# Wide key projections, shorter S words and a moved constant in a polysketch attention and expert kernel

## The chip, the cores and the metric

The kernel runs on one core of a Trainium2 chip. The metric is the device time of one execution in microseconds (us). A ratio is the mean time of one kernel's runs over the mean of the other kernel's runs of the same rounds, so it is not quite the ratio of the medians that are quoted.

## The reference, cut to what matters

```python
def phi(x):                                   # per head, R = 8
    a = np.einsum('rd,bhsd->bhsr', S1, x)
    b = np.einsum('rd,bhsd->bhsr', S2, x)
    return outer_product(a, b)                # 64 features
kv  = phi(k).T @ v ;  z = phi(k).sum(over s)
num = phi(q) @ kv  ;  den = phi(q) @ z + 1e-06
x   = (num / den), heads side by side         # 4352 x 128
# then four experts, gated: out += p[:, e] * (relu(x @ w1[e]) @ w2[e])
```

Batch 4, heads 4, sequence 1088, head dimension 32; the experts have 1024 hidden columns. S1 and S2 arrive as float64, so the kernel builds for each a leading float32 (hi) and a rest (lo) out of the bits, and projects with both.

## The kernel before

TensorE (PE) holds the 128x128 array as two halves of 64 columns and gives each half its own matmul in turn (`on_side`). The experts fill nearly all of PE's time. The attention of the next batch is cut into small "pieces" that are put between the experts' matmuls. Batch 0's keys and the first 128 rows run alone at the start, since nothing else can run yet.

The key projection, four tiles of 128 keys at a time, adds hi and lo in PSUM:

```python
for t in range(n):
    for i in range(2):              # hi, lo
        for _ in range(2):          # the two halves
            on_side(
                lambda s: _ap(kf, HP * s, HP, 32 * t, [[P, 2], [1, 32]]),
                lambda s: kT[:, P * (t0 + t) + HP * s : ... + HP],   # weights: 64 columns
                lambda s: sk[:, HP * i : HP * i + HP],               # moving: 64 columns
                start=(i == 0), stop=(i == 1))
nc.scalar.copy(<fss[b], both parts>, <kf>)
```

The first unit (`attend_first`) turns the denominators, adds 1e-6, takes the reciprocal, turns it back and multiplies:

```python
nc.vector.transpose(dT[:, 0:n], nd[0][:, 0:n])
nc.vector.tensor_scalar(out=rc, in0=<dT column>, scalar1=1e-6, scalar2=1.0, op0=ADD, op1=MULT)
nc.vector.reciprocal(rc, rc)
nc.vector.transpose(rb, <rc, repeated>)
nc.vector.tensor_tensor(out=xT, in0=nd[1], in1=rb, op=MULT)
```

Later units of queries write x to device memory and load it back turned (`xd<-y`, then `xT<-xd`); the experts of a chunk need that load.

## Time and profile before

| | before |
|---|---|
| median time | 491.54 us (491.28 to 491.69, 3 runs) |
| span of the profiled run | 489.5 us |
| first expert matmul starts | 14.16 us |
| last matmul ends | 486.15 us |
| between the two ("main part") | 471.99 us |

PE is busy in the main part but for one wait of 0.6 us. VectorE (DVE), ScalarE (ACT) and GpSimd (POOL) work beside it, so what matters is the start, the number of PE cycles in the main part, and the rare places where PE waits. The views are shown in the prediction.

### The profile page before, as it was taken

Reading aid. Unit: us, or ns where it says so; the run is one execution under the profiler, and the core shown is the slowest. Engines: PE = TensorE matmul, PEld = TensorE weight load, DVE = VectorE, ACT = ScalarE, POOL = GpSimd, SP = SyncE. Lnnn points to the kernel's source line nnn. Section 1 sums busy time; section 2 is a strip of 40 time slices with the busy share of each in tenths; the row PEclk is TensorE's granted clock in tenths of the full one; section 3 lists DMA queues with packets and bytes.
Section 4 is the critical chain, followed back from the end, with each engine's and each line's share of the span. In section 5 each row is a group of like instructions: output and inputs, shape, how many; then the busy total and the mean of one; then the engine's idle time right before and its main releaser. Section 6 shows DMA issues by size and latency. Waiting matters only on the chain.

```text
span 489.5 us, 11439 instructions
## 1 busy us (share of the span) xinstructions
PE 482.6 (99%) x4602; PEld 361.1 (74%) x4602; DVE 318.5 (65%) x746; ACT 244.4 (50%) x487; POOL 226.8 (46%) x260
## 2 busy tenths in 40 slices
PE   8999999999999999999999999999999999999997
PEld 5877777777767777555777777777777777878997
DVE  6759585868676757768675564575575666665642
ACT  3344463455445634535455464445455455566651
POOL 6052473516355444334555353444555355555570
PEclk9999999999999999999999999999999999999999
DMA  7990230040102520041102200031101200120000
GB/s 207 290 284 22 88 95 1 2 137 1 34 2 80 139 55 1 1 118 23 33 2 87 50 0 1 2 87 23 33 1 55 49 1 1 50 50 2 15 3 18
DMA packets 37588, 26.25 MB, mean 54 GB/s; under 512 B 26016, under 2 KB 34592, under 8 KB 37024
## 3 DMA queue, kind: packets, MB, share of 16 engines
q1 hardware_dynamic: 37520, 25.53, 19.0%
q8 instruction: 36, 0.59, 0.5%
q14 instruction: 16, 0.13, 0.1%
q10 hardware_dynamic: 16, 0.00, 0.0%
HBM read 21.28 MB, written 4.24 MB: 52 GB/s over the span
## 4 chain that ended last, share of the span: by engine, by line
PE 96%; DVE 2%; DMA 1%; issue 0%; ACT 0%; SPq 0%; DVEq 0%
PE h L188 49%; PE o L188 40%; PE f L188 4%; PE den L188 3%; DMA kn<-in_k_dram 1%; DVE qp L450 1%; DVE hid L698 1%; PE num L188 1%; PE h L176 0%; DVE kT L314 0%; ACT hid L723 0%; DVE qa L584 0%; ACT sh L842 0%; SPq L119 0%; DVE xT L486 0%
## 5 line engine op out<-in xcount | busy, mean ns | idle before, releaser
L188 PE MATMUL h<-xT,w_sb 128*64 128x512 f32 (+4 forms) x1408 | 300.2, 495 | 0.5 <-DVE xT L486 0.5
L698 DVE SCALAR_TENSOR_TENSOR hid<-h,hid 128x256 f32<-128x256 f32 (+6 forms) x432 | 203.6, 472 | 148.2 <-ACT hid L723 139.2
L723 ACT ACTIVATE hid<-h 128x512 f32<-128x512 f32 (+3 forms) x288 | 158.4, 550 | 195.0 <-PE h L188 157.0
L188 PE MATMUL o<-hid,w2s 128*64 128x256 f32 (+3 forms) x1152 | 221.6, 355 | 0.0
L188 PE MATMUL o<-hid,w_sb 128*64 128x256 f32 (+3 forms) x864 | 183.9, 355 | 0.0
L188 PEld LDWEIGHTS h<-xT,w_sb 128*64 128x64 f32 x1408 | 144.2, 137 | 51.8 <-issue 9.2
L188 PEld LDWEIGHTS o<-hid,w2s 128*64 128x64 f32 x1152 | 131.7, 137 | 30.9 <-issue 0.2
L838 POOL TENSOR_TENSOR ev<-yz,sh 64x256 f32<-64x256 f32 (+3 forms) x72 | 48.4, 672 | 163.5 <-ACT sh L841 160.8
L188 PEld LDWEIGHTS o<-hid,w_sb 128*64 128x64 f32 x864 | 101.0, 137 | 24.5 <-issue 6.3
L826 POOL TENSOR_TENSOR yz<-ev 128x512 f32<-128x512 f32 (+3 forms) x36 | 42.1, 1170 | 61.8 <-ACT ev L829 61.8
L838 POOL TENSOR_TENSOR ct<-ev 128x512 f32<-128x512 f32 (+3 forms) x36 | 42.0, 1167 | 2.8
L838 POOL TENSOR_TENSOR ct<-ct,gate 128x512 f32<-128x512 f32 (+3 forms) x27 | 32.1, 1189 | 2.1
L838 POOL TENSOR_TENSOR total<-total,ct 128x512 f32<-128x512 f32 (+3 forms) x27 | 31.8, 1179 | 2.1
L450 DVE TENSOR_TENSOR qp<-qa,qb 64x384 f32<-64x384 f32 (+3 forms) x44 | 32.1, 729 | 1.0
L828 ACT COPY ev<-o 128x512 f32<-128x512 f32 (+3 forms) x36 | 19.4, 539 | 11.3 <-PE o L188 10.8
L188 PE MATMUL o<-w_sb,hid 128*64 128x128 f32 x256 | 21.7, 273 | 0.0
L829 ACT COPY ev<-o 128x512 f32<-128x512 f32 (+3 forms) x36 | 19.4, 539 | 2.6
L715 ACT ACTIVATE hid<-h 128x256 f32<-128x256 f32 x24 | 9.2, 384 | 21.2 <-PE h L188 20.7
L188 PEld LDWEIGHTS o<-w_sb,hid 128*64 128x64 f32 x256 | 17.8, 137 | 2.1 <-issue 1.9
L353 DVE TENSOR_TENSOR kp<-fs 128x256 f32<-128x256 f32 (+1 forms) x24 | 14.7, 617 | 0.0
L841 ACT COPY sh<-yz 64x256 f32<-64x256 f32 (+3 forms) x36 | 13.7, 379 | 1.7 <-POOL yz L826 0.8
L842 ACT COPY sh<-yz 64x256 f32<-64x256 f32 (+3 forms) x36 | 13.7, 380 | 0.9
(113 smaller groups left out, 230.2 us busy)
## 6 DMA issues: line engine op xcount, KB each, us to landing
w_sb<-in_moe_w_dram SPq DMA_DIRECT2D x8, 512.0 KB, 7.5
gate<-gates SPq DMA_DIRECT2D x4, 1024.0 KB, 5.5
kn<-in_k_dram SPq DMA_DIRECT2D x4, 544.0 KB, 4.6
vn<-in_v_dram SPq DMA_DIRECT2D x16, 128.0 KB, 4.2
gate<-gates SPq DMA_DIRECT2D x2, 896.0 KB, 5.7
qn<-in_q_dram SPq DMA_DIRECT2D x3, 544.0 KB, 5.5
xd<-y SPq DMA_DIRECT2D x26, 48.0 KB, 1.7
out_dram<-ob SPq DMA_DIRECT2D x16, 64.0 KB, 2.0
```

Source lines behind the costliest of these rows:

```text
L188: nc.tensor.matmul(out(s), weights(s), moving(s), **flags)
L353: eng.tensor_tensor(out=_ap(kps[b], 0, P, 256 * t0 + P * p + 64 * x, [[256, n], [32, 2], [R, 4], [1, R]]), in0=_ap(src, 0, P, off + 4 * x, ...
L450: nc.vector.tensor_tensor(out=qp[p][64 * x : 64 * x + 64, 0:n], in0=qa[64 * p : 64 * p + 64, 0:n], in1=qb[64 * p : 64 * p + 64, 0:n], op=A ...
L698: nc.vector.scalar_tensor_tensor(out=out, in0=src, scalar=0.0, in1=in1, op0=ALU.max, op1=ALU.subtract)
L715: nc.scalar.activation(hd[:, 0 : 2 * n], hp[:, 0 : 2 * n], ACTF.Relu)
L723: nc.scalar.activation(hd[:, n * j : n * j + n], hp[:, 0:n], ACTF.Relu)
L826: add = lambda out, in0, in1, op=ALU.add: nc.gpsimd.tensor_tensor(out=out, in0=in0, in1=in1, op=op)
L828: nc.scalar.copy(_ap(ev, 0, P, 0, [[2 * w, 2], [1, w]]), _ap(a0, 0, P, 0, two))
L829: nc.scalar.copy(_ap(ev, 0, P, w, [[2 * w, 2], [1, w]]), _ap(a1, 0, P, 0, two))
L838: add = lambda out, in0, in1, op=ALU.add: nc.gpsimd.tensor_tensor(out=out, in0=in0, in1=in1, op=op)
L841: nc.scalar.copy(sh[HP:P, 0:w], yz[0:HP, 0, 0:w])
L842: nc.scalar.copy(sh[0:HP, 0:w], yz[HP:P, 1, 0:w])
```

## The change

Its intent is to take work off PE and off the serial start. Batches 1 to 3 project with hi and lo side by side as one 128-column moving operand, half as many matmuls, and VectorE adds the two results. The bits of S take twelve VectorE operations instead of fifteen, the copies of S are shared between ScalarE and GpSimd, and in the first unit 1e-6 enters the denominators through a matmul. One copy at the start changes place. The core of the diff:

```diff
+    def key_project_wide(b, gi, kf):
+        for t in range(n):
+            for _ in range(2):
+                on_side(
+                    lambda s: kf[half[s], P * t : P * t + P],
+                    lambda s: kT[:, P * (t0 + t) + HP * s : P * (t0 + t) + HP * s + HP],
+                    lambda s: sk[:, :],
+                    start=True, stop=True)
+        nc.scalar.copy(<fss[b]>, <hi columns of kf>)
+    def key_add(b, gi, kf):
+        nc.vector.tensor_tensor(out=fs, in0=<lo columns of kf>, in1=fs, op=ALU.add)
 ...   # keys(b): key_project -> key_project_wide, key_add one piece later
 ...   # attend_first:
+        if c == 0:
+            for _ in range(2):
+                on_side(lambda s: nd[0][half[s], 0:n],
+                        lambda s: _ap(vx, 0, P, D, [[0, HP]]),      # ones
+                        lambda s: _ap(eps, 0, P, 0, [[0, n]]),      # 1e-6 in one row
+                        start=True, stop=False)
-                    start=True,
+                    start=(i > 0 or c > 0),
+        if c:   # the tensor_scalar remains for later units only
 ...   # words: s_x, s_m, s_f by scalar_tensor_tensor (shift, then or)
 ...   # sk, sp, sr: copies split between ScalarE and GpSimd
 ...   # start():
         key_project(b, 0, kf[0])
+        key_project(b, 1, kf[1])
         next(value)
-        key_project(b, 1, kf[1])
```

More of the change, by code (lines that the diff above doesn't have):

```diff
@@ L170 @@
         nc.gpsimd.memset(own2[32 * h : 32 * h + 32, h % 2 : h % 2 + 1], 1.0)
+    eps = cpool.tile([P, 1], F32, name="eps")
+    nc.gpsimd.memset(eps[:, :], 0.0)
+    nc.gpsimd.memset(eps[0:1, :], 1e-6)
     def keep_warm(n):
@@ L200, in bits, with either @@
         nc.vector.tensor_scalar(out=out, in0=in0, scalar1=s1, scalar2=s2, op0=op0, op1=op1)
-    def either(out, a, b):
-        nc.vector.tensor_tensor(out=out, in0=a, in1=b, op=ALU.bitwise_or)
+    def either(out, in0, s1, op0, in1):
+        nc.vector.scalar_tensor_tensor(out=out, in0=in0, scalar=s1, in1=in1, op0=op0, op1=ALU.bitwise_or)
     low = _ap(s_raw, 0, R2, 0, [[2, D]])
@@ L214, with copy_on @@
     bits(s_m[:, lo], high, 31, shr, 31, shl)
+    bits(s_x[:, hi], high, 12, shl, 9, shr)
     bits(s_e[:, hi], s_f[:, hi], float(127 - 1023), ALU.add, 0.0, ALU.max)
     bits(s_e[:, lo], s_f[:, hi], float(127 - 1023 - 52), ALU.add, 0.0, ALU.max)
-    bits(s_x[:, hi], high, 12, shl, 9, shr)
-    bits(s_x[:, lo], low, 29, shr)
-    bits(s_n[:, hi], s_e[:, hi], 1.0, ALU.min)
+    either(s_x[:, hi], low, 29, shr, s_x[:, hi])
     bits(s_n[:, lo], low, 3, shl, 3, shr)
     bits(s_f[:, :], s_e[:, :], 255.0, ALU.min)
-    either(s_x[:, hi], s_x[:, hi], s_x[:, lo])
-    bits(s_e[:, :], s_f[:, :], 23, shl)
-    either(s_m[:, hi], s_x[:, hi], s_m[:, lo])
-    either(s_f[:, :], s_e[:, :], s_m[:, :])
+    either(s_m[:, hi], s_m[:, lo], 0, shl, s_x[:, hi])
+    bits(s_n[:, hi], s_e[:, hi], 1.0, ALU.min)
+    either(s_f[:, :], s_f[:, :], 23, shl, s_m[:, :])
     nc.vector.tensor_tensor(out=s_hl[0:R2, :], in0=s_n[:, :], in1=s_f[:, :].bitcast(F32), op=ALU.mult)
     nc.vector.transpose(s_T[:, :], s_hl[:, :])
+    def copy_on(scalar):
+        return nc.scalar.copy if scalar else nc.gpsimd.tensor_copy
     for h in range(H):
-        nc.scalar.copy(_ap(sk, 32 * h, 32, R2 * h, [[HP, 2], [1, R2]]), _ap(s_T, 0, 32, 0, [[D, 2], [1, R2]]))
+        copy_on(h < 2)(_ap(sk, 32 * h, 32, R2 * h, [[HP, 2], [1, R2]]), _ap(s_T, 0, 32, 0, [[D, 2], [1, R2]]))
     for i in range(3):
-        nc.gpsimd.tensor_copy(
+        copy_on(i == 2)(
             _ap(sp, 0, 32, HP * i, [[32, 2], [R, 4], [1, R]]),
@@ L240 @@
     for h in range(H):
-        nc.gpsimd.tensor_copy(
-            _ap(sr, 32 * h, 32, 32 * h, [[P, 6], [1, 32]]), _ap(sp, 0, 32, 0, [[32, 6], [1, 32]])
-        )
+        copy_on(h > 1)(_ap(sr, 32 * h, 32, 32 * h, [[P, 6], [1, 32]]), _ap(sp, 0, 32, 0, [[32, 6], [1, 32]]))
     mask_lo = [R2 + l % R2 for l in range(32)]
@@ L348, in key_project @@
         )
+    def key_project_wide(b, gi, kf):
+        t0, n = FG[gi]
+        if gi == 0:
+            fss[b] = apool.tile([P, 2, NT, 32], F32, tag="fs", name="fs")
+            kps[b] = apool.tile([P, NT, 2, P], F32, tag="kp", name="kp")
+        for t in range(n):
[4 more added lines that the diff above has]
+                    lambda s: sk[:, :],
+                    start=True,
+                    stop=True,
+                )
+        nc.scalar.copy(
+            _ap(fss[b], 0, P, 32 * t0, [[32 * NT, 2], [32, n], [1, 32]]), _ap(kf, 0, P, 0, [[32, 2], [P, n], [1, 32]])
+        )
+    def key_add(b, gi, kf):
+        t0, n = FG[gi]
+        fs = _ap(fss[b], 0, P, 32 * t0, [[32 * NT, 2], [32, n], [1, 32]])
+        nc.vector.tensor_tensor(out=fs, in0=_ap(kf, 0, P, HP, [[32, 2], [P, n], [1, 32]]), in1=fs, op=ALU.add)
     def key_product(b, t0, n, p, x, eng, kf=None):
@@ L397, in keys @@
             yield
+        kf = []
         for gi, (pool, tag) in enumerate(((ps_f, "f"), (ps_n, "den"), (ps_n, "num"))):
-            key_project(b, gi, psum(pool, tag))
+            kf.append(psum(pool, tag))
+            key_project_wide(b, gi, kf[gi])
+            if gi:
+                key_add(b, gi - 1, kf[gi - 1])
             yield
@@ L403, in keys @@
         for t0, n in ((0, 4), (4, 5)):
+            if t0:
+                key_add(b, 2, kf[2])
             for p in range(2):
@@ L460, in attend_first @@
         nd = [psum(ps_n, "den"), psum(ps_n, "num")]
+        if c == 0:
+            for _ in range(2):
+                on_side(
+                    lambda s: nd[0][half[s], 0:n],
+                    lambda s: _ap(vx, 0, P, D, [[0, HP]]),
+                    lambda s: _ap(eps, 0, P, 0, [[0, n]]),
+                    start=True,
+                    stop=False,
+                )
         for i in range(2):
@@ L474, in attend_first @@
         rc = apool.tile([P, QW // 32], F32, tag="rc", name="rc")
-        nc.vector.tensor_scalar(
-            out=rc[:, 0 : n // 32], in0=_ap(dT, 0, P, 0, [[32, n // 32]]), scalar1=1e-6, scalar2=1.0, op0=ALU.add, op1=ALU.mult
-        )
-        nc.vector.reciprocal(rc[:, 0 : n // 32], rc[:, 0 : n // 32])
+        column = _ap(dT, 0, P, 0, [[32, n // 32]])
+        if c:
+            nc.vector.tensor_scalar(
+                out=rc[:, 0 : n // 32], in0=column, scalar1=1e-6, scalar2=1.0, op0=ALU.add, op1=ALU.mult
+            )
+            column = rc[:, 0 : n // 32]
+        nc.vector.reciprocal(rc[:, 0 : n // 32], column)
         rb = apool.tile([P, UNITS[0][1]], F32, tag="rb", name="rb")
```

## The prediction

> **What bounds the kernel now.** I began with the page: busy times, then the chain that ended last.
>
> ```profile
> PE 482.6 (99%) x4602; PEld 361.1 (74%) x4602; DVE 318.5 (65%) x746; ACT 244.4 (50%) x487; POOL 226.8 (46%) x260
> ...
> PE 96%; DVE 2%; DMA 1%; issue 0%; ACT 0%; SPq 0%; DVEq 0%
> ```
>
> PE is busy for 99% and is 96% of the chain. Busy is not yet "at its rate", so I asked second for the waits of PE, and third for the instructions by form.
>
> ```profile
> PE h L176 <- DVE s_hl L212: 1.2, 1, 1.2
> PE h L188 <- DVE kT L314: 0.8, 1, 0.8
> PE den L188 <- DVE qp L450: 0.6, 1, 0.6
> PE h L188 <- DVE xT L486: 0.5, 1, 0.5
> PE den L188 <- DVE kvz L376: 0.5, 1, 0.5
> ```
>
> That is the whole list: 3.6 us, of which only the 0.6 us (a query sum at 200.35 us that waits for a product of VectorE) lies after 14.16 us. I also took each f32 form's usual start-to-start distance on one half of the array, summed these from 14.16 us on over the two halves, and got 470.2 us; from 14.16 us to the last matmul's end at 486.15 us is 472.0. So some 1.5 us at most of the main part is waiting, nearly all in the query sums. After 14.16 us only fewer PE cycles can help; before it, only what delays the first expert matmul. I read that part from the chain in order of time:
>
> ```profile
> 1.21 3.73 DMA kn<-in_k_dram
> ...
> 4.96 0.72 DVE kT L314
> ...
> 5.82 2.32 PE h L188 x72
> 8.14 0.88 PE o L188 x16
> 9.01 0.44 PE num L188 x8
> 9.45 2.12 PE f L188 x72
> ...
> 11.66 0.30 DVE kvz L376
> ...
> 12.01 0.44 PE den L188 x4
> ```
>
> Keys' load, their transposes, then solid PE from 5.82 to 11.57 us. What follows the denominators is best seen in VectorE's timeline (start, duration):
>
> ```profile
> 12.49 0.32 DVE L472 STREAM_TRANSPOSE dT<-den 128x128 f32<-128x128 f32 x1 [0.35 <-PE den L188]
> 12.85 0.17 DVE L475 TENSOR_SCALAR rc<-dT 128x4 f32<-128x4 f32 x1
> 13.05 0.18 DVE L478 RECIPROCAL rc<-rc 128x4 f32<-128x4 f32 x1
> 13.26 0.31 DVE L480 STREAM_TRANSPOSE rb<-rc 128x128 f32<-128x128 f32 x1
> 13.68 0.38 DVE L486 TENSOR_TENSOR xT<-num,rb 128x128 f32<-128x128 f32 x1
> ```
>
> This is one serial run of five operations; xT ends at 14.06 us and PE starts the first experts at 14.16. The chain view puts the 1 us before xT on the four keep-warm matmuls ("PE h L176"). I do not believe that: xT reads the numerators, done at 12.66 us, and the reciprocals, which came at 13.57 us.
>
> **What the Trainium skill says.** "Perfetto Trace Analysis", section "Identifying the Most-Contended Engine", warns that matmul busy time is a poor measure of distance to the limit. Hence my start-to-start sum; it agrees here that PE is full. "TensorE: Matmul & The Clock Gate", section "LDWEIGHTS (loading the stationary operand)", gives weight columns / 1.2 as ns: 53 ns for 64 columns. The trace fits a floor of about that size: a 64-column matmul record should take half of a 128-column one, but on one half of the array the starts are 58 ns apart against 109. That page's "Back-to-back issue gap" says the spacing is set by load and matmul together. "SBUF — State Buffer", section "Who interferes with whom", has a VectorE operation with at most one SBUF input, outside the two-port modes, not contend with GpSimd. The new sums read one PSUM and one SBUF operand. That no contention follows is not shown by the trace of before.
>
> **The change part by part.**
>
> *Wide key projections (batches 1 to 3 only; batch 0's start keeps the narrow ones).* Before, a batch has 9 tiles x 2 (hi, lo) x 2 halves = 36 matmuls of 64 columns, in the trace 72 records, f32 being recorded twice. After it has 18 matmuls of 128 columns, 36 records. The moving columns are the same; half the weight loads go. The spacing comes from these rows:
>
> ```profile
> 5.82 2.32 PE L188 MATMUL h<-sk,kT 128*64 128x64 f32 x72 [0.76 <-DVE kT L314]
> 7.94 0.31 PE L188 MATMUL o<-qT,sr 128*64 128x128 f32 x2
> ...
> 17.12 0.64 PE L188 MATMUL o<-w_sb,hid 128*64 128x128 f32 x8
> 17.56 0.64 PE L188 MATMUL h<-xT,w_sb 128*64 128x128 f32 x8
> ```
>
> 72 narrow records go from 5.82 to 7.94: 29.4 ns each with both halves working. Eight 128-column records go from 17.12 to 17.56: 0.437 us by the finer record, 54.7 ns each. Per batch 72 x 29.4 = 2.12 us becomes 36 x 54.7 = 1.97 us: 0.15 us saved, 0.44 us over three batches. It lies wholly on the PE path, so the end moves by it. This is small because hi and lo still cost their columns; the halved loads remove only the floor.
>
> *VectorE's additions.* New per batch: two of 128x256 and one of 128x64 from PSUM plus SBUF. The nearest rows are the start's products of the same operand kinds: 418 ns (128x256) and 211 ns (128x64). So 2 x 0.418 + 0.211 = 1.05 us, 3.1 us over three batches, taking VectorE from 318.5 to 321.6 us. ScalarE's copies keep their sizes (372, 372, 208 ns). All of it lies beside PE. VectorE's operations on hid idle 148 us before them, mostly for ScalarE, and the experts' second matmuls run two steps (some 6 us) behind the first, so half a microsecond in a step is absorbed. Path cost: 0.
>
> *1e-6 by a product, first unit only.* The tensor_scalar goes: from its start at 12.85 to the reciprocal's at 13.05 is 0.20 us on the serial run. Added are two 128-column matmuls into den, 4 x 54.7 = 0.22 us of PE. They need only constants and are issued after the key sums, so they run at 11.57 to 11.79 us, inside the 0.46 us in which PE waits for kvz. Net 0.20 us off the start.
>
> *Words in twelve operations.* Fifteen VectorE operations run from 2.47 to 4.44 us. Three fewer, at about 0.12 us a step (1.97 / 16 with the transpose), are 0.3 to 0.4 us. But VectorE then idles 0.52 us until the keys land at 4.94, so this only lengthens that wait: 0.
>
> *Copies of S shared between ScalarE and GpSimd.* sk is ready at 5.44 us before, sooner after. The first projection waits until 5.82 for kT. The sr copies end at 6.62 and are needed at 7.94. So 0.
>
> *Second projection's copy ahead of the first value copy.* VectorE idles 0.53 us for it before 8.70, so the products start sooner. But PE is solid through 11.57 us and the products are already in time: 0. The price is later value and qb copies on ScalarE: by its durations I get 8.95 instead of 8.41 us for the first value copy (needed at 9.25) and 10.4 instead of 9.65 for qb. The four query products, 0.29 us each, then end near 11.55 instead of 11.27, just ahead of kvz at 11.66. Up to 0.1 us of loss is possible here.
>
> Sum: 0.44 + 0.20 - 0.05 (expected part of that loss) = about 0.6 us of 491.54: 490.9.
>
> **The rivals.** First: the additions on VectorE delay hid work, PSUM banks come free later, and PE waits. For it: the three banks f, den, num are held longer, and an addition waits in the strict queue for ScalarE's copy, so hid behind it waits too. Against it: after 14 us the trace has one PE wait of consequence with VectorE at 65%, and the banks' next users come several pieces later. If each of nine additions cost PE 0.3 us, 2.7 us would go and the time would be about 493.6. Second: the start reorder backfires. If value or query copies come so late that PE's key sums stall or kvz is pushed, 0.2 to 0.5 us is lost and the gain is cancelled: 491.0 to 491.5. Third: the start gains more, because sk or the words were hidden limits on PE's first projection. The wait on kT speaks against it; at best 0.3 us more, 490.6. Fourth: the 1.5 us of query-sum waits shift, because all timing against the product pieces shifts; plus or minus 0.5 us either way.
>
> **Range and chances.** Small known terms of 0.6 us, jitter of 0.4 us between runs of before (491.28 to 491.69), and the fourth rival give 490.2 to 491.7. Two per cent would be 9.8 us: all that waits in PE is under 8 us, so faster by that is all but excluded. Slower by that would take a stall in every batch that no view hints at.
>
> **What would show it.** In the changed profile: PE projection records into f and den with 128 columns, 109 ns apart on a half, 36 per batch; PE busy lower by about 0.4 us; VectorE busy higher by 2 to 4 us; the first xT product starting near 13.48 and the first expert matmul near 13.95 us; PE's waits after that still near 0.6 us. I am wrong if the first expert matmul does not move (the keep-warm matmuls, or the query copies, set it after all), if new waits of PE for kf's banks or hid appear around 55, 155 and 275 us, or if 128-column records are spaced clearly over 109 ns.

## The result, and the profile after

| | before | after |
|---|---|---|
| median, 6 runs each | 491.51 us (491.28 to 491.89) | 490.64 us (490.54 to 491.0) |
| ratio | | 0.9983 (95%: 0.997 to 0.9996) |
| span of the profile | 489.5 us | 488.9 us |
| keys' first transpose starts | 4.96 | 5.20 |
| from it to the first expert matmul | 9.20 | 9.00 |
| main part | 471.99 | 471.24 |

The change is 0.87 us faster by the medians: inside the range, a little more than the 0.6 us that were forecast. It is far below 2%; the ratio's interval leaves out 1, but barely. The page of the changed kernel, busy time by engine and the chain by engine:

```profile
PE 482.5 (99%) x4498; PEld 358.8 (73%) x4498; DVE 322.1 (66%) x752; ACT 244.7 (50%) x488; POOL 226.6 (46%) x261
...
PE 96%; DVE 2%; DMA 1%; issue 0%; ACT 0%; SPq 0%; DVEq 0%
```

PE has 104 records fewer: 3 x 36 saved, 4 added for 1e-6. Its busy time falls by 0.1 us only, where the prediction looked for 0.4. Split by stage it does show the gain: 471.38 us become 470.63 in the main part, but the warm-up matmuls took 4.26 instead of 3.86 us in this profile, and the rest of the start 7.58 instead of 7.36, which is the product for 1e-6. VectorE's busy time rises by 3.6 us, of which the additions are 3.1. Groups of VectorE by form (count, busy us and mean ns, idle before):

```profile
L377 DVE TENSOR_TENSOR fs<-f,fs 128x256 f32<-128x256 f32 x3 | 1.2, 414 | 0.0
L377 DVE TENSOR_TENSOR fs<-den,fs 128x256 f32<-128x256 f32 x3 | 1.2, 414 | 0.0
...
L377 DVE TENSOR_TENSOR fs<-num,fs 128x64 f32<-128x64 f32 x3 | 0.6, 215 | 0.0
```

The serial run at the end of the start, in VectorE's timeline of the changed kernel:

```profile
12.73 0.32 DVE L516 STREAM_TRANSPOSE dT<-den 128x128 f32<-128x128 f32 x1 [0.34 <-PE den L193]
13.08 0.18 DVE L525 RECIPROCAL rc<-dT 128x4 f32<-128x4 f32 x1
13.29 0.31 DVE L527 STREAM_TRANSPOSE rb<-rc 128x128 f32<-128x128 f32 x1
13.71 0.38 DVE L533 TENSOR_TENSOR xT<-num,rb 128x128 f32<-128x128 f32 x1
```

From dT to xT's product it is 0.98 us now and was 1.19. The product starts at 13.71 although the last keep-warm matmul ends only at 13.87: the keep-warm matmuls, which the chain view of before had in this place, do not set it. The whole start is later in this profile all the same, since the keys landed 0.24 us later; the experiments show how far this moves by itself.

The projections themselves, PE's timeline of before around the first group of batch 3 (four tiles), and then of the changed kernel:

```profile
274.65 1.10 PE L188 MATMUL f<-sk,kT 128*64 128x64 f32 x29
275.59 0.38 PE L188 MATMUL o<-hid,w_sb 128*64 128x256 f32 x1
```

```profile
274.15 1.10 PE L193 MATMUL f<-sk,kT 128*64 128x128 f32 x15
275.03 0.38 PE L193 MATMUL o<-hid,w_sb 128*64 128x256 f32 x1
```

On the half that starts first, 16 narrow records take 0.94 us (58 ns each) and eight wide ones 0.88 (109 ns each). That is 0.06 us for four tiles, and by the finer starts 0.129 us for the nine tiles of a batch. Three times that is 0.39 us, but the main part is 0.75 us shorter. Where the other 0.36 us come from was the open question.

### The profile page after: what moved, and what is told of

Read it like the earlier page. It is cut to its first block, busy times and chain, and to the rows that moved or that the text cites. A ratio compares the mean times of both kernels' runs of the same rounds, so it can differ in the third digit from the quotient of the medians.

```text
span 488.9 us, 11239 instructions
## 1 busy us (share of the span) xinstructions
PE 482.5 (99%) x4498; PEld 358.8 (73%) x4498; DVE 322.1 (66%) x752; ACT 244.7 (50%) x488; POOL 226.6 (46%) x261
## 4 chain that ended last, share of the span: by engine, by line
PE 96%; DVE 2%; DMA 1%; issue 0%; ACT 0%; SPq 0%; DVEq 0%
PE h L193 49%; PE o L193 40%; PE f L193 4%; PE den L193 2%; DMA kn<-in_k_dram 1%; DVE qp L485 1%; DVE hid L745 1%; PE num L193 0%; PE h L181 0%; DVE kT L319 0%; ACT hid L770 0%; DVE qa L631 0%; ACT sh L889 0%; SPq L119 0%; DVE xT L533 0%
## 5 line engine op out<-in xcount | busy, mean ns | idle before, releaser
L485 DVE TENSOR_TENSOR qp<-qa,qb 64x384 f32<-64x384 f32 (+3 forms) x44 | 33.4, 758 | 1.0
```

The source lines that it names most:

```text
L485: nc.vector.tensor_tensor(out=qp[p][64 * x : 64 * x + 64, 0:n], in0=qa[64 * p : 64 * p + 64, 0:n], in1=qb[64 * p : 64 * p + 64, 0:n], op=A ...
```

## The experiments

Eleven kernels ran; all gave correct results. In the table, "start" is from the keys' first transpose to the first expert matmul, "main" from there to the last matmul's end, both in the one profile of that kernel.

| run | median (runs) | ratio to before (95%) | start | main |
|---|---|---|---|---|
| e1 wide only | 490.82 (5) | 0.9982 (0.9969 to 0.9994) | 9.20 | 471.24 |
| e2 1e-6 only | 491.30 (5) | 0.9993 (0.998 to 1.0005) | 9.00 | 471.86 |
| e3 words and copies only | 491.70 (5) | 0.9998 (0.9986 to 1.0011) | 9.20 | 472.07 |
| e4 order only | 491.56 (5) | 0.9997 (0.9983 to 1.0011) | 9.24 | 472.31 |
| e5 all but wide | 491.43 (5) | 0.9994 (0.998 to 1.0008) | 9.00 | 472.18 |
| e6 narrower still | 497.87 (4) | 1.0126 (1.0112 to 1.014) | 9.21 | 478.15 |
| e7 additions x 4 | 490.58 (4) | 0.9977 (0.9964 to 0.9991) | 9.44 | 470.91 |
| e8 before again | 491.77 (5) | 1.0003 (0.999 to 1.0015) | 9.71 | 472.38 |
| e9 before, shifted | 492.77 (4) | 1.0033 (1.0015 to 1.0052) | 9.51 | 471.83 |
| e10 after, shifted | 491.56 (4) | 0.9999 (0.9984 to 1.0014) | 9.70 | 471.24 |
| e11 sums later | 490.90 (6) | 0.9982 (0.997 to 0.9995) | 9.00 | 471.35 |

The medians of before in the same rounds were 491.56 (e1 to e4), 491.63 (e5 to e8), 491.69 (e9, e10) and 491.71 us (e11).

### Each part alone

e1 takes only the wide projections with their additions:

```diff
 ...   # key_project_wide and key_add as in the change
-            key_project(b, gi, psum(pool, tag))
+            kf.append(psum(pool, tag))
+            key_project_wide(b, gi, kf[gi])
+            if gi:
+                key_add(b, gi - 1, kf[gi - 1])
```

> Only the wide key projections with their additions, the start as before. My theory: the whole gain of this part is on PE's path. 36 records of 128 columns at 109 ns on a half replace 72 of 64 columns at 58 ns: 0.13 to 0.15 us a batch, 0.4 us in all. The two traces so far suggest up to 0.75 us from the first expert matmul to the last matmul (471.99 us before, 471.24 after), so 0.4 to 0.75 us faster than before, and the start not earlier. Rival A (the start made most of the gain): 0 to 0.2 us faster. Rival B (the additions on VectorE hold PE up): slower, with new waits of PE in the three key stretches.

It was 0.74 us faster by the medians, the start stayed at 9.20 us and the main part was 471.24 us, exactly that of the changed kernel. Rivals A and B fall: the main part's whole gain is in this edit, and no new wait appeared.

e2 takes only the product for 1e-6:

```diff
+        if c == 0: <two matmuls of ones by eps into nd[0], start=True, stop=False>
-        nc.vector.tensor_scalar(out=rc, in0=<dT>, scalar1=1e-6, ...)
-        nc.vector.reciprocal(rc, rc)
+        nc.vector.reciprocal(rc, <dT>)          # c == 0 only
```

> Only the 1e-6 by a product in the first unit. My theory: 0.20 us faster, because one operation of 0.20 us from start to start leaves the serial run from the denominators to xT; from the end of the keys' load to the first expert matmul 9.0 us instead of 9.22. Rival (the keep-warm matmuls set the start of xT's product, as the chain view has it): 0, with xT's product still starting just after the fourth keep-warm matmul ends.

The start fell from 9.20 to 9.00 us and xT's product began at 13.77 us, before the last keep-warm matmul ended at 13.94. The time is 0.26 us lower, within its noise; the 0.20 us is what the trace shows.

e3 and e4 take the words with the copies, and the order of the copies:

```diff
-        nc.scalar.copy(<sk, h>)                 # e3: sk, sp and sr shared, words in twelve
+        copy_on(h < 2)(<sk, h>)
-        next(value)                             # e4
         key_project(b, 1, kf[1])
+        next(value)
```

> Only the words in twelve operations and the shared copies of S. My theory: 0 (within 0.1 us): the transposed S is ready some 0.4 us earlier, VectorE waits that much longer for the keys, and PE's first projection still follows the keys' transpose by 0.14 us. Rival A: the copies of sk were a hidden limit, then 0.2 to 0.4 us faster, with PE's first projection closer to the keys' transposes.

> Only the order at the start: second projection's copy ahead of the first value copy. My theory: 0 within 0.1 us: PE runs without a gap from the first projection to the last key sum, and the query products still end before kvz. Rival: it loses up to 0.1 us where the query products end later than PE's key sums, or gains where the key products held PE's key sums (then fewer us from the first projection to the last key sum than 5.75).

Both left the time where it was. In e3 the turned S was ready at 4.05 us instead of 4.44, and VectorE then waited 1.17 us for the keys instead of 0.52 (0.26 of it because they landed later in this profile). In e4 the query products ended at 11.45 us and kvz started at 11.89: the loss of up to 0.1 us that the prediction allowed for did not come.

e5 is the changed kernel with the narrow projections back:

```diff
-        kf = []
 ...
-            kf.append(psum(pool, tag))
-            key_project_wide(b, gi, kf[gi])
-            if gi:
-                key_add(b, gi - 1, kf[gi - 1])
+            key_project(b, gi, psum(pool, tag))
 ...   # and the last key_add goes too
```

> The changed kernel with only the wide projections undone (and the additions with them). My theory: 0.2 us faster than the kernel before (the product's part alone), so 0.4 to 0.75 us slower than the changed kernel. Rival A (the start made most of the gain): 0.6 to 0.9 us faster than before.

It kept the 0.20 us of the start (9.00) and lost the main part's gain: 0.20 us faster than before by the medians. So the parts add up. What e3, e4 and e5 also show is a main part between 472.07 and 472.31 us, longer than before's 471.99, while the two kernels with wide projections had 471.24 both times.

### The floor under a narrow matmul

e6 makes the narrow projections narrower, with the same columns in all:

```diff
+            for p in range(2):                            # batches 1 to 3
                 for i in range(2):
                     for _ in range(2):
-                        moving sk[:, HP * i : HP * i + HP]                # 64 columns
+                        moving sk[:, HP * i + 32 * p : HP * i + 32 * p + 32]   # 32 columns
```

> The kernel before with each 64-column key projection of batches 1 to 3 split into two of 32 columns: 72 matmuls, 144 records a batch, moving columns unchanged, results right. My theory (the load of the 64 weight columns sets a floor of some 58 ns on a half): the 32-column records are also about 58 ns apart, a batch costs 144 x 58 / 2 = 4.2 us instead of 2.1, and the kernel is 6.3 us slower. Rival (no floor, each record has a fixed cost of about 5 ns besides its columns, 53 ns for 64): 32 columns take 27 + 5 = 32 ns, a batch 2.3 us, and the kernel is 0.5 us slower.

The two theories were a factor of ten apart, and the run gave 6.24 us more by the medians, against 6.3 expected of the floor. The 32-column records are 58 ns apart on a half, exactly as the 64-column ones. By form (x count):

```profile
L188 PE MATMUL f<-sk,kT 128*64 128x32 f32 x192 | 6.8, 222 | 0.0
L188 PE MATMUL den<-sk,kT 128*64 128x32 f32 x192 | 6.6, 222 | 0.0
```

So a record of 32 moving columns costs the same 58 ns as one of 64. That this is the load of its 64 weight columns is what the Trainium skill's 53 ns suggests ("TensorE: Matmul & The Clock Gate", section "LDWEIGHTS (loading the stationary operand)"); the run shows the floor, not its cause.

### The additions on VectorE

e7 does each addition four times, three into a spare tile:

```diff
+        for _ in range(3):
+            nc.vector.tensor_tensor(out=<spare>, in0=<lo columns of kf>, in1=fs, op=ALU.add)
         nc.vector.tensor_tensor(out=fs, in0=<lo columns of kf>, in1=fs, op=ALU.add)
```

> The changed kernel with each of its nine additions on VectorE done four times, three into a spare tile that nobody reads; results right. VectorE gets 3 x 3.1 = 9.4 us more work in the key stretches. My theory (the additions lie beside PE): the same as the changed kernel within 0.2 us, 0.7 to 0.9 us faster than before. Rival B (the additions hold hid and the banks up): slower by a part of the 9.4 us, 1 us or more, with waits of PE on VectorE's hid or key products in the key stretches.

VectorE's busy time rose to 329.9 us. Three of four additions are not the change's, and with them the rival's sign does appear once, in the key stretch of batch 2. From PE's list of waits:

```profile
PE h L193 <- DVE hid L751: 0.3, 1, 0.3
```

This wait of 0.26 us is at 172.5 us; the changed kernel has none there. VectorE's timeline just before it, in the changed kernel and in e7:

```profile
167.74 0.87 DVE L382 TENSOR_TENSOR kp<-fs 128x320 f32<-128x320 f32 x1
168.53 1.14 DVE L745 SCALAR_TENSOR_TENSOR hid<-h,hid 128x512 f32<-128x512 f32 x2
```

```profile
169.96 1.43 DVE L388 TENSOR_TENSOR kp<-fs 128x320 f32<-128x320 f32 x1
171.31 1.14 DVE L751 SCALAR_TENSOR_TENSOR hid<-h,hid 128x512 f32<-128x512 f32 x2
```

The hid work comes 2.8 us later (0.2 of it from the later start), behind four additions in place of one and behind key products that took longer (1.43 instead of 0.87 us here). By the starts of ScalarE's activations of hid, counted from the first expert matmul, PE's stream loses 0.51 us there against the changed kernel's. So VectorE's slack is not without end. With one addition each there is no such step, and the 1 us or more of the rival did not come.

The main part came out 0.33 us shorter than the changed kernel's all the same: near 199 us e7 gains 0.84 us, by luck. The place is one query product. The changed kernel, VectorE's and GpSimd's timelines near 198 us:

```profile
198.17 1.62 DVE L485 TENSOR_TENSOR qp<-qa,qb 64x384 f32<-64x384 f32 x1
...
198.10 1.27 POOL L873 TENSOR_TENSOR yz<-ev 128x512 f32<-128x512 f32 x1 [1.57 <-ACT ev L876]
```

and the same two operations in e7:

```profile
198.87 0.56 DVE L491 TENSOR_TENSOR qp<-qa,qb 64x384 f32<-64x384 f32 x1
...
198.97 1.60 POOL L879 TENSOR_TENSOR yz<-ev 128x512 f32<-128x512 f32 x1 [1.72 <-ACT ev L882]
```

In both pairs the one that starts second is stretched: the product, of two SBUF operands, from 0.56 to 1.62 us, or the GpSimd addition from 1.27 to 1.60. PE's only wait of the main part in the changed kernel (0.6 us on both halves) hangs on that product; e7's was late enough by then to swap the order. The Trainium skill has this in "SBUF — State Buffer", section "Who interferes with whom": a VectorE instruction with two SBUF inputs contends with a GpSimd instruction that reads SBUF. The trace agrees. The additions of the change, with one operand in PSUM, took 414 ns both with a GpSimd operation beside them (at 61.53 us) and without (58.48 us).

### Noise, and a transfer met by an instruction fetch

e8 is the kernel before, unchanged.

> The kernel before, against itself: the noise of this measurement, expected within 0.1 us of 0, and a second profile of it. I want to see how much the landing of the keys' load (4.94 us in the first profile of before, 5.17 in that of the changed kernel) moves by itself: 0.1 to 0.3 us expected.

The medians differ by 0.14 us, a little over what was expected, and its runs spread from 491.43 to 492.33. The keys' first transpose, which follows their landing at once, began at 4.98 us here and at 4.95 to 5.51 us over all thirteen profiles. A larger part was elsewhere. The first projections of e8, in PE's timeline:

```profile
5.84 2.80 PE L188 MATMUL h<-sk,kT 128*64 128x64 f32 x72 [0.20 <-POOL sr L241]
```

The same 72 records took 2.32 us in the first profile of before. The trace's record of the full granted clock begins only at 6.95 us in e8 and at 4.33 us in that first profile, though the warm-up matmuls are the same and start at 1.19 us in both. Up to 6.95 us the records of a half start 107 ns apart, and 58 ns after it. So the start of e8 is 9.71 instead of 9.20 us, with nothing changed. The 9.44 us of e7 have the same cause (full clock at 6.76 us).

The main part was 472.38 us in e8 and 471.99 before. I laid the activations of hid of all kernels side by side. Among the kernels with 64-column projections nearly all agree to 0.1 us or better until the chunk of experts that begins near 134 us; there each is late by its own amount, and the kernels with wide projections are not. That chunk waits for the reload of x. The DMA queue's timeline (SP) of before and of the changed kernel:

```profile
126.27 1.74 SPq L550 DMA_DIRECT2D xd<-y  x4
131.22 0.34 SPq L558 DMA_DIRECT2D xT<-xd  x1
```

```profile
126.15 1.74 SPq L597 DMA_DIRECT2D xd<-y  x4
129.23 0.34 SPq L605 DMA_DIRECT2D xT<-xd  x1
```

The stores of x begin at the same time, the reload is issued 2 us later before, because it waits for the last store. In the view of DMA queues for 127.5 to 131.5 us, before (packets, MB, share of the engines' time) has, and the changed kernel lacks, the first of these lines:

```profile
q8 instruction: 1, 0.02, 2.1%
q14 instruction: 1, 0.01, 0.6%
```

One packet of 16 KB, from 128.7 us for 1.4 us: a fetch of instructions. The last eight packets of the stores start as it ends (130.04 us) and finish at 130.4 us, all others by 128.9; that these eight share its DMA engine is read from this. In the changed kernel all are done at 128.8. The Trainium skill describes such fetches, in 16 KiB blocks of 256 instructions on the sequencers' own DMA queues ("Runtime: NRT & Kernel Launch", section "Instruction fetch mechanics"), and calls their cost mostly hidden. In all six profiles with narrow projections of 64 columns (before, e2 to e5, e8) this packet starts between 127.9 and 129.6 us and the reload is issued at 131.0 to 132.0 us; in the three with wide ones (after, e1, e7) the packets lie at 119 and 134 us and the reload at 129.2 to 129.4. To tell chance from effect, e9 and e10 lengthen PE's instruction stream early on and touch nothing else:

```diff
-    keep_warm(10)                               # ten of 512 columns
+    for _ in range(55):
+        wp = psum(ps_h, "h")
+        nc.tensor.matmul(wp[0:64, 0:93], warm[:, 0:64], warm[:, 0:93], start=True, stop=True)
```

> The kernel before, with its ten warm-up matmuls of 512 columns replaced by 55 of 93 columns (weights of 64 columns): about the same warm-up time, 45 matmuls and their weight loads more in PE's instruction stream, nothing else. In all six profiles with narrow projections in which I looked, a 16 KB instruction packet runs from some 128 to 131 us beside the store and reload of x, the reload of x is issued at 131.0 to 132.0 us and the chunk that starts near 134 us is late by up to 0.4 us; in the three wide ones the packet falls at 119 and 134 us, the reload is issued at 129.2 to 129.4 us and nothing waits. My theory: the fetch of instructions collides by chance with this transfer, and the change's shorter PE stream moved it away; so with some 90 instructions more the packet comes some 5 us earlier, near 123 to 125 us, the reload is issued near 129.3 us, and from the first expert matmul to the last one's end it takes 471.8 to 471.9 us rather than up to 472.4. Rival (the narrow projections themselves delay the reload, through PE or VectorE): reload still at 131 us or later.

> The changed kernel with the same 55 short warm-up matmuls in place of ten. My theory: the instruction packet that fell at 133.6 us now falls some 5 us earlier, near 128.5 us, collides with the store of x, the reload is issued at 131 us or later, and the chunk near 134 us starts 0 to 0.4 us late: from the first expert matmul to the last one's end 471.25 to 471.7 us instead of 471.24. Rival: reload still at 129.3 us.

The queue's timelines of e9 and of e10:

```profile
127.14 1.74 SPq L552 DMA_DIRECT2D xd<-y  x4
130.23 0.34 SPq L560 DMA_DIRECT2D xT<-xd  x1
```

```profile
126.87 1.73 SPq L599 DMA_DIRECT2D xd<-y  x4
131.32 0.34 SPq L607 DMA_DIRECT2D xT<-xd  x1
```

Both moved as forecast. In e9 the packet began at 123.1 us, the reload was issued 3.09 us after the first store's issue (127.14 to 130.23; before 4.95, after 3.08), and with narrow projections the main part was 471.83 us, 0.16 less than before. In e10 the packet began at 128.4 us and met the stores; the reload came 4.45 us after them, at 131.32 us. The rivals fall: the delay follows the fetch and not the projections. In e10 it cost nothing: counted from the first expert matmul, the reload's last packet ended at 118.4 us and PE comes to this chunk at 119.3 us (in the changed kernel 133.48 - 14.19). In the others it ended at 118.81 (e2), 119.05 (before), 119.13 (e3), 119.24 (e5), 119.33 (e4) and 119.44 us (e8), and PE can start only some 0.6 us after it (in e4 133.72 to 134.30). In both profiles the start is longer because the 55 matmuls took longer: the first projection began at 6.67 and 6.78 us instead of 5.82 and 6.05. e9's times spread more than that, 492.1 to 494.49 us, and its profile is of the fastest; what the slower ones lost was not looked into.

Against e9, whose reload was in time, the other narrow kernels lost 0.04 (e2), 0.16 (before), 0.24 (e3), 0.35 (e5), 0.48 (e4) and 0.55 us (e8) by the end, 0.30 us on average: the same order in which their reloads ended. (Up to 0.1 us of e3's loss arose earlier, near 24 us.) before and e8 are the same kernel, so 0.39 us of this is chance between two executions. The wide kernels lost nothing; three of them have 471.24 us. Without the delay the difference of narrow and wide streams is 471.83 - 471.24 = 0.59 us, on the narrow side from one profile.

### A try for more

I took from e7's main part that the wait near 199 us is worth 0.3 us; by the activations it is 0.84, but e7 had lost 0.51 before. e11 moves the query sums one piece later in the changed kernel:

```diff
         qT = query_turn(b, c, n)
         yield
         yield
-        yield
 ...
                 query_product(qp, p, x, n, qa, qb)
                 yield
         yield
         yield
+        yield
```

> The changed kernel with the query sums one piece later (one of the three empty pieces after the queries' transpose moved to behind the query products; the count of pieces unchanged). In the traces of before and of the changed kernel one query product near 198 to 200 us takes 1.62 us instead of 0.55, beside a GpSimd addition of 1.27 us, and PE waits 0.6 us for it on both halves; in the run with four times the additions it took 0.56 us, PE did not wait, and the main part took 470.91 us instead of 471.24. My theory: that wait is the only one left after the first experts, so with the sums one piece later the main part takes 470.9 us, 0.3 us less than the changed kernel, and the time is near 490.3 us. Rival: moving the pieces makes another product meet a GpSimd addition or delays a reload of x, and nothing or less than nothing is won: 490.6 us or more.

The wait did go from PE's list, but the main part was 471.35 us, 0.11 more than the changed kernel's, and the median 490.90. The rival was right: by the activations the stream was 0.35 to 0.49 us behind the changed kernel's after the first key stretch and 0.61 to 0.77 us near 132 us. The sums won 0.84 us near 200 us, and some of that was lost again before 235 us. What caused these losses was not looked into. No version here clearly beats the changed kernel: e7's 490.58 us is within the noise of 490.64, and it carries useless work.

## Why the prediction was right

**The product for 1e-6: right in size and place.** 0.20 us forecast; in each of after, e2 and e5 the start is 0.20 us shorter, and dT to xT's product 0.98 instead of 1.19 us. The reading that the keep-warm matmuls were not the cause, against the chain view, held. That xT's product began at 13.71 and not 13.48 us, and the experts at 14.19 and not 13.95, is the later landing of the keys.

**Words, copies of S, order at the start: zero, as forecast.** e3 and e4 show it. The expected 0.05 us of loss from later query products did not occur; they end 0.4 us ahead of kvz.

**Additions on VectorE: zero on the path, as forecast.** 1.04 us a batch (2 x 0.414 + 0.215) against 1.05 forecast. The reasoning, that a delay in hid work is absorbed, held at this size and not without limit: four times as many cost PE 0.51 us in one of three batches (e7).

**Wide projections: the mechanism right, the size too small.** This is the mis-sized term of the sum: "0.15 us saved, 0.44 us over three batches" measured 0.59 us where no transfer disturbs (e9 against after). By the activations batch 1 gave 0.16 us, as forecast, and batches 2 and 3 gave 0.21 each. The two stream rates account for 0.39 us of it. (The forecast's 0.15 is 0.02 above these rates: the 2.12 us that it read for 72 records include a first distance of 78 ns.) The rest, 0.20 us, is seen in the finer starts: when both halves work on narrow records they fall into step, starting 1 to 2 ns apart, and on the way one half once has distances of 88 and 108 ns instead of 58 (in before at 278.2 us; 83 and 107 at 155.0). Summed over the key stretches of batches 2 and 3, starts came 89 and 131 ns later than the usual distances in before, and 14 and 55 ns in the changed kernel: 75 and 76 ns less for each, the mean of both halves. With 129 ns of rate that makes 0.205 us a batch, against 0.215 and 0.213 between the kernels' matching events. e9's trace has the same late starts. That falling into step is the cause was read from the traces; no experiment changed it alone. For batch 1 the finer starts could not be assigned to halves.

**What was missed: the reload of x.** The prediction said that nearly all of some 1.5 us of waiting in the main part lies in the query sums, though its list showed 0.6 us there (they are worth 0.84, by e7), and its fourth rival had only those shift. In fact kernels with narrow projections lost another 0.04 to 0.55 us where an instruction fetch met a transfer, and before was one of them with 0.16. So 0.16 of the 0.75 us in the main part is luck of where the fetch fell: a side effect of a shorter instruction stream and not of narrow or wide matmuls. With warm-up matmuls e9 took the delay of the reload away, and e10 brought it back, there without loss. The list of PE's waits hardly showed it, because one half of the array was still working while the other waited: the gap that both halves shared was 0.12 us in e4, which its list leaves out, and 0.19 in e8, whose list puts it down to ScalarE.

The sum, profile against profile: 0.20 at the start, 0.75 in the main part (0.59 and 0.16), less 0.24 for the later landing of the keys and 0.06 for a longer tail after the last matmul, makes 0.65 us; the spans differ by 0.66. In the timed runs these last terms vary by themselves, and 0.87 us with an interval of about 0.2 to 1.5 us (from the ratio) agrees.

## What to carry to other kernels

A float32 record on half the array with 64 weight columns took 58 ns here with 32 moving columns as with 64, so splitting below 64 gains nothing and joining two of 64 into one of 128 gains 6%, small beside an engine that streams for 470 us. When an engine is full, find gains by distances between fixed events, or by busy time stage by stage, not by busy time of the whole, and when a difference is larger than the rates explain, compare event by event until the place where it appears. Half a microsecond can come from where an instruction fetch happens to fall, so test such a difference with an edit that moves only the fetch.

## What the Trainium skill lacked or had wrong

- "TensorE: Matmul & The Clock Gate" has the weight load by its columns (53 ns for 64). The runs show a floor of 58 ns for float32 records of 64 and of 32 columns on a half (e6). No page says that narrow matmuls on two halves fall into step, with single distances of 88 and 108 ns on the way.
- "Runtime: NRT & Kernel Launch" calls the cost of an instruction fetch mostly hidden. It does not say that the packet can delay a transfer: here the reload of x was issued 4.95 us after the stores' issue instead of 3.08 us, and kernels lost up to 0.55 us in the main part.
- "SBUF — State Buffer" has the contention of VectorE and GpSimd right; it names two slowdowns (6.8 and 1.5 times) without the operations' sizes. Here one product of 64x384 grew from 0.56 to 1.62 us, 2.9 times, beside a GpSimd addition of 1.27 us.
- No page says that a list of an engine's waits can leave out a wait of one half of PE's array; the chunk near 134 us was 0.3 us late in e4 (against before) and PE's list shows no such wait, while that of the weight loads shows 0.5 us there.
